# Banded attention and MoE on one core: half of the first k by another queue, v of batch 0 in four loads, and a new order of the first batch's attention

## The chip, the core and the metric

The kernel runs on one core of a Trainium2 chip. The metric is the device time of one execution in microseconds. The kernel before takes 321.01 us (median of three runs, 320.98 to 322.28). Profiles are of one further execution; the one of the kernel before took 319.8 us, of which 318.1 lie between its first and last instruction, with a mean granted TensorE clock of 0.994.

## What is computed

Two layers, one after the other. The first is attention over a local sequence of 512 tokens and 32 global tokens, for 8 batches and 8 heads of dimension 64: global queries see every key, local queries see the global keys and a band of 32 keys to each side. The second is a feed-forward layer of width 2048 with the gate x * sigmoid(1.702 x).

```python
k_all = concat([k_g, k_l]);  v_all = concat([v_g, v_l])
out_g = softmax(scale * q_g @ k_all.T) @ v_all
s_ll  = where(|i - j| <= 32, scale * q_l @ k_l.T, -1e9)
out_l = softmax(concat([scale * q_l @ k_g.T, s_ll])) @ v_all
x     = heads side by side of concat([out_g, out_l])      # 4352 x 512
h     = x @ w_in                                          # 512 x 2048
out   = (h * sigmoid(1.702 * h)) @ w_out                  # 2048 x 512
```

Inputs and output are f32 in DRAM. The kernel computes in bf16 with f32 sums.

## The kernel before

Four heads of one batch make a "quad", so each batch has two: quads 0 and 1 are batch 0. A quad is worked off in steps: `Tk`, `Tq` transpose k and q on VectorE in blocks of 32; `S(rnd)` are the score matmuls of one half of the keys, `X` their exp on ScalarE, `M` the band mask on VectorE; `K` and `XK` are scores and exp for the global keys; `U(0)` sums the rows, `U(1)` and `U(2)` multiply by v; `R` makes the reciprocal of the row sums; `XL` writes the normalised result, which is the operand of the MoE matmuls; `Gm` and `G` do the same for the global queries. The MoE matmuls of w_in are `h_mm` and those of w_out `o_mm`.

Most loads are issued by GpSimd, whose DMAs cast f32 to bf16 on the way. SyncE and ScalarE issue plain copies only. The loads at the start:

```python
def load_k(b, u, j):                      # one of 4 heads of quad u: 32 partitions, 64 KB in bf16
    nc.gpsimd.dma_start(out=loaded[b][0][32 * j : 32 * j + 32, u], in_=kf[b, j][:, u])

def load_v(b, us=(0, 1)):                 # 4 loads each: 64 KB for one quad, 128 KB for both
    s = slice(us[0], us[-1] + 1)
    hs = slice(4 * us[0], 4 * us[-1] + 4)
    for t in (0, 2, 1, 3):
        p = slice(32 * t, 32 * t + 32)
        nc.gpsimd.dma_start(out=vtiles[b % 2][p, s, :, :, :D], in_=vf[b, t][:, hs])

load_g32(0, "qk")                         # q_g, k_g as f32, by SyncE
q32 = ld.tile([128, 16 * D], F32, name="q32", bufs=1)
nc.scalar.dma_start(out=q32, in_=qf[0][:, 0])     # q of quad 0 as f32, by ScalarE
load_g32(0, "v", eng=nc.scalar)
load(0, kq=False)
for j in range(4):
    load_k(0, 0, j)                       # k of quad 0
# ... two affine_selects on GpSimd for the band mask ...
load(0, (1,))                             # k and q of quad 1
# ...
keep(17, psP.tile([128, 512], F32, name="w", tag="p"))    # matmuls on zeros at the start

def load_rest():
    load_v(0, (0,))
    load_v(0, (1,))
    for part in range(2):
        cs = slice(part * (d_ff // 2), (part + 1) * (d_ff // 2))
        for u in range(2):
            nc.gpsimd.dma_start(out=w_in_sb[:, part, 2 * u : 2 * u + 2, :], in_=w_in_r[u][:, :, cs])
    # ... w_out, and k, q and v of batches 1 and 2
```

The loaded half of w_in that belongs to quad 0's result (`kc` 0 and 1) is the first of these four, that of quad 1 (`kc` 2 and 3) the second; the last two are the columns of `fc` 8 to 15. PSUM has eight banks: four in one tile for scores (`psS`, one buffer), four single ones (`psP`), which are used in turn for `kb`, the three `ov`, `og` and later for `hp`.

The order of the first batch:

```python
a, c = Quad(0), Quad(1)
make_mb()
for hf in range(2):
    nc.scalar.activation(rq[:, 0, ...], q32[:, ...], AF.Copy)     # cast q, halves of 512
make_mask()
cast_g32(0, "qk"); transpose_g(0, 2); a.ext()
a.Tq(0, 8); a.Tq(8, 16); a.Tk((0, 1)); a.Tk((2, 3))
load_rest()
a.S(0); a.X(0); expand_g(0, 0)
a.S(1, split=True, warm=4); a.X(1)        # 4 further matmuls on zeros ahead
c.ext(); cast_g32(0, "v"); c.Tk(); expand_g(0, 1)
a.K(); a.XK(); a.M(0); c.Tq()
c.S(0); c.X(0); a.M(1)
load_g32(1, "qkv", hold=True)
a.U(0); a.U(1)
c.S(1); c.X(1)
a.U(2); c.K(); c.XK()
a.Gm(); a.R(); c.M(0); a.XL(0); a.XL(1); c.M(1); a.G()
pt = pts[0] = psS.tile([128, 4, 512], F32, name="s4")
for fc in (0, 1):
    h_mm(0, fc, pt[:, fc, :], (0, 1))     # the first MoE matmuls
for unit in range(3):
    c.U(unit)
for fc in (2, 3):
    h_mm(0, fc, pt[:, fc, :], (0, 1))
c.R(); c.XL(0); c.XL(1); c.Gm()
for kc in (2, 3):
    for fc in range(4):
        h_mm(0, fc, pt[:, fc, :], (kc,))
# ... tanh, c.G(), gate, then fc 4 to 15, then the further batches
```

Of the kernel before, what the change touches and what calls it, by code (L numbers as in the profile page):

```python
# [12 lines left out]
F32 = mybir.dt.float32  # L13
BF16 = mybir.dt.bfloat16
FP8 = mybir.dt.float8e4
AF = mybir.ActivationFunctionType
# [4 lines left out]
def kernel(  # L21
# [12 lines left out]
    nc = tc.nc  # L34

    B, H, Sl, D = q_l.shape
# [20 lines left out]
    ld = ctx.enter_context(tc.tile_pool(name="ld", bufs=3))  # L57
# [7 lines left out]
    kf = k_l.rearrange("b (u j) (c r t) d -> b j r u c (t d)", j=4, c=4, t=4)  # L65
# [7 lines left out]
    def load(b, us=(0, 1), kq=True):  # L73
        if b not in loaded:
            loaded[b] = (ld.tile([128, 2, 4, 4 * D], BF16, name="rk"),
                         ld.tile([128, 2, 16 * D], BF16, name="rq"))
        if kq:
            for j in (0, 2, 1, 3):
                for u in us:
                    load_k(b, u, j)  # L80
            load_q(b, us)

    def load_k(b, u, j):
        nc.gpsimd.dma_start(out=loaded[b][0][32 * j : 32 * j + 32, u], in_=kf[b, j][:, u])  # L84

    def load_q(b, us):
        s = slice(us[0], us[-1] + 1)
        nc.gpsimd.dma_start(out=loaded[b][1][:, s], in_=qf[b][:, s])
# [3 lines left out]
    def load_v(b, us=(0, 1)):  # L92
# [5 lines that stand above are left out]
# [12 lines left out]
    def load_g32(b, names, hold=False, eng=None):  # L110
        for name, s in (("q", qgf), ("k", kgf), ("v", vgf)):
            if name in names:
                t = g32[b, name] = consts.tile([128, 2, D], F32, name="g32%s%d" % (name, b))
                if hold:
                    nc.vector.memset(t[:, :, 0:1], 0.0)
                (eng or nc.sync).dma_start(out=t, in_=s[:, 2 * b : 2 * b + 2, :])

    def cast_g32(b, names):
        for name, t in (("q", rqg), ("k", rkg), ("v", rvg)):
            if name in names:  # L120
                if b:
                    nc.scalar.activation(t[:, 2 * b : 2 * b + 2, :], g32[b, name], AF.Copy)
                else:
                    nc.vector.tensor_copy(t[:, 2 * b : 2 * b + 2, :], g32[b, name])

    load_g32(0, "qk")

    q32 = ld.tile([128, 16 * D], F32, name="q32", bufs=1)
    nc.scalar.dma_start(out=q32, in_=qf[0][:, 0])
    load_g32(0, "v", eng=nc.scalar)  # L130
    load(0, kq=False)
    for j in range(4):
        load_k(0, 0, j)


    mk = consts.tile([32, 208], BF16)
# [1 line left out]
    for sg, base in ((1, 2 * W + 3), (-1, -3)):  # L138
        nc.gpsimd.affine_select(
            out=mk, in_=mk, pattern=[[-sg, 208]], compare_op=ALU.is_ge,  # L140
            fill=0.0, base=base, channel_multiplier=4 * sg,
        )
    load(0, (1,))

    w_in_sb = wts.tile([128, 2, NKC, d_ff // 2], BF16)
    w_out_sb = wts.tile([128, FC, d_model], BF16)
# [24 lines left out]
    def make_mb():  # L171
        for k in range(4):
            nc.vector.tensor_copy(mb[32 * k : 32 * k + 32],
                                  mk[:, 3 - k : 195 - k].rearrange("p (r t) -> p t r", t=16))

    def make_mask():
        at = 0
        for c, (r0, nr) in enumerate(WIN):
            lo = r0 - 8 * c + 2
            nc.scalar.activation(  # L180
                mask[:, c // 2, at : at + 16 * nr].rearrange("p (t r) -> p t r", t=16),
                mb[:, :, lo : lo + nr], AF.Copy)
            at = (at + 16 * nr) % LW
# [7 lines left out]
    for i in range(2):  # L191
        v = consts.tile([128, 2, 4, 4, D + 2], BF16, name="v%d" % i)
# [14 lines left out]
    def transpose_g(lo, hi):  # L207
        for dst, s in ((kgT, rkg), (qgT, rqg)):
            nc.vector.transpose(dst[:, lo:hi, :32], s[:, lo:hi].bitcast(F32))

    def expand_g(b, which):
        qs = slice(2 * b, 2 * b + 2)
        kgBD, vgBD = GB[b % 3]
        out_, in_ = (kgBD, kgT[:, qs].bitcast(BF16)) if which == 0 else (vgBD[:, :, :, :D], rvg[:, qs])
        nc.vector.tensor_mul(
            out_,
            in_.rearrange("p n (o w) -> p n o w", o=1).to_broadcast([128, 2, 4, D]),
            bdm.rearrange("p (o j) w -> p o j w", o=1).to_broadcast([128, 2, 4, D]),
        )

    def load_rest():
        load_v(0, (0,))
        load_v(0, (1,))
        for part in range(2):
            cs = slice(part * (d_ff // 2), (part + 1) * (d_ff // 2))
            for u in range(2):
                nc.gpsimd.dma_start(out=w_in_sb[:, part, 2 * u : 2 * u + 2, :], in_=w_in_r[u][:, :, cs])
        for g4 in range(4):
            nc.gpsimd.dma_start(
                out=w_out_sb[:, 4 * g4 : 4 * g4 + 4, :].rearrange("p (g e) m -> p g (e m)", e=2),  # L230
                in_=w_out_r[:, 2 * g4 : 2 * g4 + 2, :])
            if g4 == 1:
                load(1, (0,))
        load(1, (1,))
        load_v(1, (0,))
        load_v(1, (1,))
        load(2)
# [173 lines left out]
    def width(i):  # L411
        return TB if i < B else B * Sg
# [3 lines left out]
    def h_mm(i, fc, hp, kcs):  # L416
        for kc in kcs:
            nc.tensor.matmul(hp[:, : width(i)], lhsT=w_in_c[:, fc // 8, kc, fc % 8 // 2, :, fc % 2],  # L418
                             rhs=(xL[i] if i < B else xG)[:, kc, :],
                             start=(kc == 0), stop=(kc == NKC - 1))  # L420
# [45 lines left out]

    a, c = Quad(0), Quad(1)
    rk, rq = loaded[0]
    make_mb()
    for hf in range(2):  # L470
        nc.scalar.activation(rq[:, 0, 512 * hf : 512 * hf + 512], q32[:, 512 * hf : 512 * hf + 512], AF.Copy)
    make_mask()
    cast_g32(0, "qk")
    transpose_g(0, 2)
    a.ext()
    a.Tq(0, 8)
    a.Tq(8, 16)
    a.Tk((0, 1))
    a.Tk((2, 3))
    load_rest()  # L480
    a.S(0)
    a.X(0)
# [1 line left out]
    a.S(1, split=True, warm=4)  # L484
    a.X(1)
    c.ext()
    cast_g32(0, "v")
    c.Tk()
    expand_g(0, 1)
    a.K()  # L490
    a.XK()
    a.M(0)
    c.Tq()
    c.S(0)
    c.X(0)
    a.M(1)
    load_g32(1, "qkv", hold=True)
    a.U(0)
    a.U(1)
    c.S(1)  # L500
    c.X(1)
    a.U(2)
    c.K()
    c.XK()
    a.Gm()
    a.R()
    c.M(0)
    a.XL(0)
    a.XL(1)
    c.M(1)  # L510
    a.G()
    gTs[0] = moe.tile([128, FC, TB], BF16, name="gT")
    pt = pts[0] = psS.tile([128, 4, 512], F32, name="s4")
    for fc in (0, 1):
        h_mm(0, fc, pt[:, fc, :], (0, 1))
    for unit in range(3):
        c.U(unit)
    for fc in (2, 3):
        h_mm(0, fc, pt[:, fc, :], (0, 1))
    c.R()  # L520
    c.XL(0)
    c.XL(1)
    c.Gm()
    for kc in (2, 3):
        for fc in range(4):
            h_mm(0, fc, pt[:, fc, :], (kc,))
    th4 = th4s[0] = ld.tile([128, 4, TB], F32, name="th4", bufs=1)

    def tanh2(hf):
# [24 lines left out]
    a, c = nq[1]  # L554
# [37 lines left out]
    a, c = nq[2]  # L592
# [116 lines left out]
```

The softmax here doesn't subtract the row's maximum and nothing guards it: scores larger than these inputs give would overflow.

## Time and profile before

| | |
|---|---|
| time, median of three | 321.01 us |
| span of the profiled execution | 318.1 us |
| TensorE (PE) busy | 305.9 us, 96% |
| VectorE (DVE) busy | 214.9 us, 68% |
| ScalarE (ACT) busy | 165.9 us, 52% |
| GpSimd (POOL) busy | 81.0 us, 25% |
| first score matmul | 8.34 us |
| first v load issued by GpSimd | 7.34 us |
| first w_in load issued by GpSimd | 12.58 us |
| first MoE matmul | 20.52 us |

The profile counts time from the first instruction. Issuing a DMA takes time on the engine that issues it; the data land later. A row of the timeline merges equal instructions that follow each other, and gives in brackets how long the engine was idle ahead of it and what ended that. Matmuls with output `s` are scores on line 297, and on line 418 the first four column blocks of the MoE, since both use the same PSUM tile. Idle time of TensorE counts here: its busy share is 96%, and it is at nine tenths or more in every slice from the fifth to the last but one.

### The profile page before, as it was taken

The numbers are of one execution on the slowest core, as the hardware profiler recorded it, in microseconds if no ns is written. First come the engines' busy times: TensorE is split into PE (matmuls) and PEld (weight loads), VectorE is DVE, ScalarE is ACT, GpSimd is POOL, SyncE is SP. The second block draws the span as 40 slices with busy tenths as digits, with TensorE's granted clock in tenths as the row PEclk, the third lists the DMA queues.
The fourth block names the chain that finished last, engine by engine and source line by source line (L and its number), as shares of the span: only waits on it lengthen the run. The fifth ranks groups of instructions, "written<-read, shape, count | busy, mean of one in ns | idle before, by whom it ended". The sixth has DMA issues, their size and how long they took to land.

```text
span 318.1 us, 7343 instructions
## 1 busy us (share of the span) xinstructions
PE 305.9 (96%) x2997; PEld 148.3 (47%) x2997; DVE 214.9 (68%) x467; ACT 165.9 (52%) x252; POOL 81.0 (25%) x133
## 2 busy tenths in 40 slices
PE   8759999999999999999999999999999999999994
PEld 2424444544554455444454455445454454445651
DVE  8847876978865876677866876687758855573320
ACT  4723765276446744565536735564546642563421
POOL 8932579585136000910045001200000000000000
PEclk9989999999999999999999999999999999999999
DMA  8999999999959211970269111900110011101122
GB/s 155 125 169 209 207 155 174 176 150 126 154 79 172 40 34 44 142 116 1 68 69 179 22 35 51 116 2 20 48 44 26 2 35 51 50 0 34 35 66 66
DMA packets 59904, 27.40 MB, mean 86 GB/s; under 512 B 43232, under 2 KB 51424, under 8 KB 59872
## 3 DMA queue, kind: packets, MB, share of 16 engines
q0 software_dynamic: 51568, 17.11, 50.4%
q1 hardware_dynamic: 7888, 9.25, 10.7%
q10 hardware_dynamic: 416, 0.59, 0.6%
q8 instruction: 23, 0.38, 0.5%
q14 instruction: 9, 0.07, 0.1%
HBM read 35.13 MB, written 8.91 MB: 138 GB/s over the span
## 4 chain that ended last, share of the span: by engine, by line
PE 89%; POOL 3%; DMA 2%; DVE 2%; ACT 1%; issue 1%; POOLq 0%; DVEq 0%; ACTq 0%
PE op L443 36%; PE hp L418 35%; PE s L297 5%; PE ov L353 4%; PE ov L345 4%; DMA w_in_sb<-in_moe_w_in_dram 2%; PE kb L330 2%; POOL v L97 2%; POOL rk L84 1%; PE s L418 1%; PE og L371 1%; PE s L306 1%; DVE sT L377 0%; DVE gT L462 0%; ACT th L425 0%
## 5 line engine op out<-in xcount | busy, mean ns | idle before, releaser
L443 PE MATMUL op<-w_out_sb,gT 128*128 128x512 bf16 x544 | 125.2, 379 | 0.4 <-DVE xL L386 0.4
L426 DVE SCALAR_TENSOR_TENSOR gT<-th,hp 128x512 bf16<-128x512 f32 (+1 forms) x140 | 91.1, 656 | 47.4 <-ACT th L425 46.8
L418 PE MATMUL hp<-xL,w_in_sb 128*128 128x512 bf16 x496 | 108.5, 379 | 0.0
L425 ACT ACTIVATE th<-hp 128x512 f32<-128x512 f32 (+1 forms) x140 | 79.8, 573 | 42.5 <-PE hp L418 39.4
L418 PEld LDWEIGHTS <-w_in_sb 128*128 128x128 bf16 x576 | 56.1, 98 | 67.6 <-DMA w_in_sb<-in_moe_w_in_dram 3.6
L443 PEld LDWEIGHTS <-gT 128*128 128x128 bf16 x544 | 51.9, 98 | 61.0 <-issue 3.6
L318 ACT ACTIVATE e<-s 128x1712 bf16<-128x1712 f32 x31 | 49.5, 1597 | 29.3 <-PE s L297 25.4
L97 POOL DMA_DIRECT2D v<-in_v_l_dram x40 | 28.9, 730 | 95.9 <-PE og L371 91.0
L450 ACT ACTIVATE ob<-op 128x512 f32<-128x512 f32 x34 | 20.3, 597 | 62.8 <-PE op L443 62.8
L84 POOL DMA_DIRECT2D rk<-in_k_l_dram x64 | 34.9, 553 | 17.3 <-DMA w_in_sb<-in_moe_w_in_dram 6.3
L325 DVE TENSOR_TENSOR e<-e,mask 128x1408 bf16<-128x1408 bf16 x32 | 28.0, 874 | 11.1 <-ACT e L318 11.0
L377 DVE STREAM_TRANSPOSE sT<-ov 128x512 f32<-128x512 f32 x16 | 11.4, 714 | 25.3 <-PE ov L353 25.3
L297 PE MATMUL s<-q,kT 32*128 32x200 bf16 (+1 forms) x512 | 21.2, 283 | 1.5 <-DVE q L270 0.7
L386 DVE TENSOR_TENSOR xL<-ov,rs 128x512 bf16<-128x512 f32 x32 | 20.6, 685 | 1.5
L297 PEld LDWEIGHTS <-kT 32*128 32x128 bf16 x512 | 10.8, 95 | 11.7 <-issue 7.5
L353 PE MATMUL ov<-e,v 128*32 128x192 bf16 (+1 forms) x512 | 15.6, 243 | 0.0
L353 PEld LDWEIGHTS <-v 128*32 128x32 bf16 x512 | 12.1, 99 | 3.7 <-issue 0.5
L345 PE MATMUL ov<-ek,vgBD 128*32 128x512 bf16 x128 | 12.9, 393 | 0.3 <-DVE sT L377 0.3
L381 DVE STREAM_TRANSPOSE rs<-rT 128x512 f32<-128x512 f32 x16 | 11.4, 712 | 0.5
L267 DVE STREAM_TRANSPOSE kT<-rk 128x512 f32<-128x512 f32 (+1 forms) x17 | 11.3, 668 | 0.0
L270 DVE STREAM_TRANSPOSE q<-rq 128x512 f32<-128x512 f32 (+1 forms) x17 | 10.8, 643 | 0.1
L330 PE MATMUL kb<-q,kgBD 128*128 128x512 bf16 x32 | 9.8, 388 | 0.5 <-ACT e L316 0.5
(64 smaller groups left out, 149.5 us busy)
## 6 DMA issues: line engine op xcount, KB each, us to landing
out_dram<-ob SPq DMA_DIRECT2D x136, 64.0 KB, 1.9
rk<-in_k_l_dram POOLq DMA_DIRECT2D x64, 64.0 KB, 4.0
rq<-in_q_l_dram POOLq DMA_DIRECT2D x6, 512.0 KB, 6.8
v<-in_v_l_dram POOLq DMA_DIRECT2D x24, 128.0 KB, 4.4
w_in_sb<-in_moe_w_in_dram POOLq DMA_DIRECT2D x4, 512.0 KB, 12.3
w_out_sb<-in_moe_w_out_dram POOLq DMA_DIRECT2D x4, 512.0 KB, 13.4
v<-in_v_l_dram POOLq DMA_DIRECT2D x16, 64.0 KB, 3.7
rq<-in_q_l_dram POOLq DMA_DIRECT2D x3, 256.0 KB, 7.9
```

The costliest lines, as they stand in the source:

```text
L84: nc.gpsimd.dma_start(out=loaded[b][0][32 * j : 32 * j + 32, u], in_=kf[b, j][:, u])
L97: nc.gpsimd.dma_start(out=vtiles[b % 2][p, s, :, :, :D], in_=vf[b, t][:, hs])
L297: nc.tensor.matmul(ps[j][:, off : off + n * nr], lhsT=self.k[p, 128 * c : 128 * c + 128, e], rhs=self.q[p, t0 : t0 + n, r0 : r0 + nr, e], ...
L318: nc.scalar.activation(e[:, :, :RW], self.ps[:, :, :RW], AF.Exp, scale=scale)
L325: nc.vector.tensor_mul(e, e, mask[:, rnd : rnd + 1, :].to_broadcast([128, 4, LW]))
L345: nc.tensor.matmul(ov[32 * j : 32 * j + 32, :], lhsT=lv, rhs=self.ek, start=True, stop=False, skip_group_check=True)
L353: nc.tensor.matmul(ov[32 * j : 32 * j + 32, :].rearrange("p (t r) -> p t r", t=16)[:, :, r0 : r0 + nr], lhsT=lv, rhs=self.E[c // 2][:, j, ...
L386: nc.vector.tensor_mul(self.x[:, 2 * self.u + h, :], self.st[1 + h], self.st["rs"])
L418: nc.tensor.matmul(hp[:, : width(i)], lhsT=w_in_c[:, fc // 8, kc, fc % 8 // 2, :, fc % 2], rhs=(xL[i] if i < B else xG)[:, kc, :], start=( ...
L425: nc.scalar.activation(th[:, :n], hp[:, :n], AF.Tanh, scale=0.851)
L426: nc.vector.scalar_tensor_tensor(gTs[i][:, fc, :n], in0=th[:, :n], scalar=1.0, in1=hp[:, :n], op0=ALU.add, op1=ALU.mult)
L443: nc.tensor.matmul(op, lhsT=gTs[i][:, fc, tci * 128 : tci * 128 + 128], rhs=w_out_sb[:, fc, :], start=(first and fc == 4 * f4), stop=(fc = ...
```

## The change

K of quad 0 no longer comes through GpSimd with a cast, but as f32 through SyncE's queue, in four loads; ScalarE casts one half of its columns and VectorE the other. The small global q and k move from SyncE's queue to ScalarE's, behind q. The eight v loads of batch 0 become four of twice the size. GpSimd thereby has fewer loads to issue before those of w_in. The order of the first batch is changed as well: both score rounds of quad 1 come ahead of the products of quad 0 with v, all of quad 1's U ahead of the first MoE matmuls, and the global results (`G`, `Gm` of quad 1) behind them.

```diff
-    load_g32(0, "qk")
-
+    load(0, kq=False)
     q32 = ld.tile([128, 16 * D], F32, name="q32", bufs=1)
+    k32 = ld.tile([128, 4, 4 * D], F32, name="k32", bufs=1)
     nc.scalar.dma_start(out=q32, in_=qf[0][:, 0])
-    load_g32(0, "v", eng=nc.scalar)
-    load(0, kq=False)
     for j in range(4):
-        load_k(0, 0, j)
+        nc.sync.dma_start(out=k32[32 * j : 32 * j + 32], in_=kf[0, j][:, 0])
+    load_g32(0, "qk", eng=nc.scalar)
+    load_g32(0, "v")
+    for j in range(4):
+        load_k(0, 1, j)
 # ... affine_selects
-    load(0, (1,))
+    load_q(0, (1,))
 # ... in load_rest()
-        load_v(0, (0,))
-        load_v(0, (1,))
+        load_v(0)
 # ... the order of batch 0; cast_q(hf) is the former loop's body
     make_mb()
-    for hf in range(2):
-        nc.scalar.activation(rq[:, 0, ...], q32[:, ...], AF.Copy)
+    cast_q(0)
+    cast_q(1)
+    nc.scalar.activation(rk[:, 0, 2:4], k32[:, 2:4], AF.Copy)
     make_mask()
     cast_g32(0, "qk")
     transpose_g(0, 2)
     a.ext()
+    nc.vector.tensor_copy(rk[:, 0, 0:2], k32[:, 0:2])
     a.Tq(0, 8)
+    a.Tk((0, 1))
     a.Tq(8, 16)
-    a.Tk((0, 1))
     a.Tk((2, 3))
 # ... load_rest, a.S(0), a.X(0), expand_g, a.S(1), a.X(1)
     c.ext()
-    cast_g32(0, "v")
-    c.Tk()
-    expand_g(0, 1)
+    c.T()
     a.K()
     a.XK()
     a.M(0)
-    c.Tq()
     c.S(0)
     c.X(0)
+    cast_g32(0, "v")
+    expand_g(0, 1)
     a.M(1)
     load_g32(1, "qkv", hold=True)
     a.U(0)
-    a.U(1)
+    c.K()
+    c.XK()
+    a.R()
     c.S(1)
     c.X(1)
+    a.U(1)
     a.U(2)
-    c.K()
-    c.XK()
     a.Gm()
-    a.R()
     c.M(0)
+    c.M(1)
     a.XL(0)
     a.XL(1)
-    c.M(1)
-    a.G()
 # ... gTs[0], pt
-    for fc in (0, 1):
-        h_mm(0, fc, pt[:, fc, :], (0, 1))
     for unit in range(3):
         c.U(unit)
-    for fc in (2, 3):
+    c.R()
+    for fc in range(4):
         h_mm(0, fc, pt[:, fc, :], (0, 1))
-    c.R()
     c.XL(0)
     c.XL(1)
-    c.Gm()
     for kc in (2, 3):
         for fc in range(4):
             h_mm(0, fc, pt[:, fc, :], (kc,))
+    a.G()
+    c.Gm()
```

## The prediction

> **What bounds the kernel now.** I read the slices first (TensorE at nine tenths or more from the fifth slice on), then the list of TensorE's waits, the timeline of the first 28 us, and the same stretch in windows. One TensorE wait is far longer than the rest:
>
> ```profile
> PE s L418 <- DMA w_in_sb<-in_moe_w_in_dram: 3.4, 1, 3.4
> PE w L155 <- DVE warm L151: 1.5, 1, 1.5
> PE s L297 <- DVE q L270: 0.7, 1, 0.7
> ...
> PE ov L345 <- DVE sT L377: 0.3, 1, 0.3
> ```
>
> TensorE is busy 305.9 of 318.1 us, and only 0.7 us of named waits lie after 27 us (0.3 on sT, 0.4 on xL). Whatever is won must therefore be won before the first MoE matmuls. In the timeline (start, length, engine, line, what, in brackets the idle time ahead and its releaser):
>
> ```profile
> 1.35 2.29 POOL L84 DMA_DIRECT2D rk<-in_k_l_dram  x4 [0.84 <-POOLq L693]
> ...
> 4.52 2.27 POOL L84 DMA_DIRECT2D rk<-in_k_l_dram  x4
> ...
> 7.34 5.25 POOL L97 DMA_DIRECT2D v<-in_v_l_dram  x8
> ...
> 8.34 0.66 PE L297 MATMUL s<-q,kT 32*128 32x200 bf16 x16 [0.17 <-DVE kT L267]
> ...
> 12.58 2.80 POOL L227 DMA_DIRECT2D w_in_sb<-in_moe_w_in_dram  x4
> ...
> 20.52 1.50 PE L418 MATMUL s<-xL,w_in_sb 128*128 128x512 bf16 x4 [3.43 <-DMA w_in_sb<-in_moe_w_in_dram]
> ```
>
> GpSimd issues without a pause from 1.35 us, and reaches w_in only at 12.58. The weights land 7.9 us later, and TensorE has run out of attention work by then. It stands still until 20.52, and pays twice: the windows show what the clock did (length, then busy time per engine, PEclk, DMA share, GB/s):
>
> ```profile
> 18.00:20.00 2.00, 0.00 (x0) 0.00 (x0) 0.93 (x4) 0.00 (x0) 0.00 (x0) 1.00 1.01 159
> 20.00:22.00 2.00, 1.48 (x8) 0.41 (x12) 0.00 (x0) 0.00 (x0) 0.55 (x1) 0.74 1.14 209
> 22.00:24.00 2.00, 2.00 (x45) 1.46 (x48) 0.76 (x2) 0.00 (x0) 0.00 (x0) 0.50 1.13 205
> 24.00:26.00 2.00, 2.00 (x52) 0.91 (x40) 1.86 (x4) 0.00 (x0) 0.54 (x1) 0.91 1.13 206
> ```
>
> Lost clock: 2 x (0.26 + 0.50 + 0.09) = 1.7 us. So at most 3.4 + 1.7 = 5.1 us hang on this one transfer. The last of the 16 first MoE matmuls (two halves of w_in over four column blocks) ends at 27.9 us; from there on TensorE is full. I predict how far that moment moves.
>
> **What the Trainium skill says.** "TensorE: Matmul & The Clock Gate", Part 1, says that an idle window of about 3.4 us puts the array on half its clock, until a busy window of that length has passed. The trace agrees: 3.43 us of idleness, then clock 0.50. "DMA: Bandwidth & Descriptors", Issuing engines are not separate DMA queues: a load from another queue uses the same 16 DMA engines and saves only issue time. The trace shows those engines loaded from 4 us on (DMA share 1.0 to 2.1 per window), so I don't count the earlier issue in full. "VectorE: DVE Perf Modes", What auto-detection actually checks: a one-source operation between SBUF tensors can run two elements per cycle; by that the new 128x512 cast might take half of what one element per cycle would. The trace has only 128x128 casts, at 0.22 to 0.35 us, which don't decide it.
>
> **The change, part by part.**
>
> 1. *GpSimd's issue time.* Four k loads leave its queue (2.27 us). Eight v loads of 64 KB become four of 128 KB. The eight took 5.25 us; the later 128 KB v loads take 0.78 us each, so four take 3.1: 2.1 us less. w_in is issued at about 12.6 - 2.3 - 2.1 = 8.2 us.
>
> 2. *The DMA engines.* What lies ahead of w_in stays almost the same in bytes read: k's first half merely comes as f32, 512 KB written instead of 256. v's rows arrive as 128-byte packets, 0.52 MB, and the windows from 10 to 14 us move 117 to 143 GB/s while it is at work, so v needs about 4 us however it is issued, beginning when q of quad 1 is in. I put that at 7.5 to 8 us instead of about 10, and v's end at about 12 instead of 14.7. So w_in's data move 2.5 us earlier (1.6 to 3.4), not 4.4. In the timeline GpSimd[...] is let go by w_in at 20.76, 24.79, 27.65 and 30.16; these stand for the four landings. After: about 18.2, 22.3, 25.2, 27.7.
>
> 3. *The front.* q32 (512 KB on ScalarE's queue) now shares the engines with k32, and q_g and k_g are second and third on ScalarE's queue instead of first and second on SyncE's. Before, ScalarE began its cast of q at 4.72, and VectorE its cast of q_g at 5.96 without a wait. I estimate both small tensors and k32 at 6.3 to 7 us: up to 0.3 us of wait. VectorE gets one more cast (128x512, f32 to bf16) ahead of the transposes: 0.35 to 0.6 us, I take 0.5. The three transposes ahead of the first scores stay three. The first scores start at 8.34 + 0.3 + 0.5 = **9.15 us**. ScalarE's added cast (0.61 us, as its q casts) lies in its idle time before the first exp.
>
> 4. *The middle, TensorE's new order.* Times from the rows of before. exp of quad 0, first half: 9.85 to 11.45 (1.60). c.T is moved up on VectorE and its data are on the chip sooner, so its two 0.71 us transposes end at 11.75; then the mask (0.9) to 12.65. exp, second half: 11.45 to 13.2 (1.81, overlapped a little); mask to 14.15; exp of the kg scores to 13.75. Scores of quad 1 start at 12.5 on TensorE, the row sums of quad 0 (U 0) at 13.9, ended by the mask at 14.6. exp of quad 1: 13.75 to 15.3; kg exp to 15.9; second scores of quad 1 at 15.35 to 16.25; exp to 18.1. TensorE fills this time with U 1, U 2 and Gm of quad 0 (0.8 + 0.8 + 0.5), to 18.4. VectorE: mask of quad 1 at 17.95 to 18.85, then the two xL products (1.3) to 20.15. Quad 1's U 0 ends at 19.3; U 1 and U 2 need the PSUM banks that the xL products free (19.5, 20.15) and end at 21.2. ScalarE and VectorE thus set the pace here; TensorE loses about 1 us in small gaps, none near 3.4 us.
>
> 5. *The first MoE matmuls.* Eight on quad 0's xL: 21.2 to 22.95 (0.216 each). They want the first w_in at 21.2, and it is there at 18.2. VectorE meanwhile: R of quad 1 (1.7) to 21.85, xL to 22.5 and 23.15. The last eight run 22.95 to 24.7 and want the second w_in, there at 22.3. G of both quads now comes after them, and Gm of quad 1 is put behind (0.5). Equal work is done at **25.2 us instead of 27.9: 2.7 us less**. The next two w_in pieces are wanted at about 25.2 + 4 x 0.87 = 28.7, and the last is there at 27.7.
>
> Afterwards nothing changes in kind: the later streams move by 2.5 us, TensorE's demand by 2.7. 321.0 - 2.7 = **318.3 us**, 0.8% less.
>
> **Rivals.** (a) *The wait only moves*: w_in comes no earlier, as the DMA engines are the limit. For it: DMA shares of 1 and over from 4 us on. Against: in 6 to 10 us they move only 127 to 134 GB/s while GpSimd is at full issue, so issue limits there. Even then the first w_in (20.5) is in time for the new order, while the second (24.8) and the last (30.2) are 1.8 us late: about 320 us. (b) *The front gets dearer than counted*: k32 or k_g land at 8 us; the scores start at 10, and the chain through exp shifts by as much: 319 to 319.5. (c) *ScalarE and VectorE are not as tight as I laid them*, or later starts overlap better: up to 4.5 us gained, 316.5. (d) *The DMA queue falls behind later*, at q and v of batch 1 (v lands late, U at 51 us wants it): some tenths of a us back.
>
> **Range and chances.** The middle is 318.3. (a), (b) and (d) pull up by 1 to 1.7, (c) down by 1.5; eight in ten lie in 316.9 to 319.9. Over 2% faster would be under 314.6, more than the 5.1 us at stake plus the small gaps: 0.02. Over 2% slower would take a new wait of 6 us that nothing points to: 0.01. Within 2%: 0.97.
>
> **What the profile after would show.** Right: no TensorE wait for w_in over 0.5 us, and no clock of 0.50 after the start; the v issues in one row of four, about 3.1 us; w_in issued near 8.2; first scores near 9.15; a cast of k on VectorE of about 0.5 us; the last matmul on L418 with output s at about 24.7 and more exp-bound gaps ahead of it. Wrong: a wait for w_in in front of the second eight matmuls or at the eighth column block (rival a); VectorE idle before 7.5 us on k32 or k_g (rival b); waits for v or rq between 38 and 60 us (rival d).

## The result and the profile after

The changed kernel takes **319.5 us** (median of four runs, 319.07 to 319.67) against 321.01. The ratio is 0.9941, with a 95% interval of 0.9915 to 0.9968; it is estimated from the runs of both kernels and is not the quotient of these two medians (0.9953). The predicted 318.3 lay below the result, the range of 316.9 to 319.9 holds it. The gain was 1.5 us by the medians, 1.9 by the ratio (1.0 to 2.7 over its interval), instead of 2.7. TensorE no longer waits for w_in, as predicted, but the front of the kernel became longer than predicted.

TensorE's waits of the changed kernel, longest first (the columns are total us, times, longest):

```profile
PE s L298 <- DVE q L271: 2.8, 1, 2.8
PE w L157 <- DVE warm L153: 1.5, 1, 1.5
PE ov L354 <- DVE e L326: 0.9, 1, 0.9
PE ov L346 <- ACT ek L337: 0.6, 1, 0.6
```

The wait for w_in is gone. In its place stands one of 2.8 us ahead of the first scores. The timeline of the changed kernel shows both ends of the trade:

```profile
5.08 3.22 POOL L97 DMA_DIRECT2D v<-in_v_l_dram  x4
...
7.86 0.49 DVE L124 CAST rkg<-g32k 128x128 bf16<-128x128 f32 x1 [1.04 <-DMA g32k<-in_k_g_dram]
...
8.47 2.81 POOL L228 DMA_DIRECT2D w_in_sb<-in_moe_w_in_dram  x4 [0.17 <-issue]
...
8.61 0.63 ACT L477 ACTIVATE rk<-k 128x512 bf16<-128x512 f32 x1 [2.10 <-DMA k<-in_k_l_dram]
...
9.18 0.42 DVE L482 CAST rk<-k 128x512 bf16<-128x512 f32 x1
...
10.65 0.90 PE L298 MATMUL s<-q,kT 32*128 32x200 bf16 x16 [2.76 <-DVE q L271]
...
11.49 1.89 PE L157 MATMUL s<-warm 128*128 128x512 bf16 x4
...
23.49 3.63 PE L419 MATMUL s<-xL,w_in_sb 128*128 128x512 bf16 x16
```

GpSimd reaches w_in at 8.47 instead of 12.58 us. But k_g has landed only at 7.86 and k, as f32, at 8.61; VectorE's casts and transposes follow, and the first scores start at 10.65 instead of 8.34. TensorE, whose zero matmuls end at 7.9, is idle for 2.76 us, and the windows (length, busy time per engine, PEclk, DMA share, GB/s) show the clock that follows:

```profile
8.00:10.00 2.00, 0.00 (x0) 0.00 (x0) 1.93 (x10) 1.39 (x5) 1.83 (x4) 1.00 1.51 187
10.00:12.00 2.00, 1.34 (x18) 0.81 (x19) 2.00 (x9) 0.59 (x2) 1.48 (x3) 0.54 2.42 154
12.00:14.00 2.00, 2.00 (x21) 0.61 (x20) 1.59 (x3) 1.20 (x1) 1.76 (x3) 0.61 1.67 195
14.00:16.00 2.00, 1.39 (x24) 0.63 (x21) 0.79 (x4) 1.94 (x5) 0.56 (x2) 1.00 1.13 212
```

The half clock, which before lay in the windows from 20 to 26 us, now lies in those from 10 to 14: the first scores take 0.90 us instead of 0.66, the four zero matmuls 1.89 instead of 1.04. So the column blocks from fc 4 on, which started at 27.77 us before, start at 27.33 in this profile. This pair of profiles shows a smaller gain than the medians do: 0.2 us (319.8 to 319.61). The profiled execution of the kernel before is 1.2 us faster than its median. Its mean clock was 0.994; in 39 further runs of that kernel the clock lay between 0.982 and 0.995, with a median of 0.989, so most of them lose more to the clock than the profile shows.

### The profile page after: what moved, and what is told of

It reads as the page before. It is cut to its first block, busy times and chain, and to the rows that moved or that the text cites. A ratio compares the mean times of both kernels' runs of the same rounds, so it can differ in the third digit from the quotient of the medians.

```text
span 317.9 us, 7344 instructions
## 1 busy us (share of the span) xinstructions
PE 305.5 (96%) x2997; PEld 148.0 (47%) x2997; DVE 216.0 (68%) x468; ACT 166.5 (52%) x253; POOL 77.1 (24%) x125
## 4 chain that ended last, share of the span: by engine, by line
PE 84%; DMA 10%; POOL 2%; DVE 1%; issue 1%; ACT 0%; POOLq 0%; DVEq 0%
PE op L444 36%; PE hp L419 33%; DMA w_out_sb<-in_moe_w_out_dram 6%; PE s L298 5%; PE ov L354 4%; PE ov L346 3%; PE kb L331 2%; DMA v<-in_v_l_dram 2%; DMA rq<-in_q_l_dram 2%; POOL rk L84 1%; PE og L372 1%; PE s L307 1%; DVE sT L378 0%; POOL mk L141 0%; DVE rs L382 0%
## 5 line engine op out<-in xcount | busy, mean ns | idle before, releaser
L319 ACT ACTIVATE e<-s 128x1712 bf16<-128x1712 f32 x31 | 49.6, 1599 | 27.9 <-PE s L298 24.5
L97 POOL DMA_DIRECT2D v<-in_v_l_dram x36 | 27.1, 765 | 97.7 <-PE og L372 93.7
L84 POOL DMA_DIRECT2D rk<-in_k_l_dram x60 | 32.7, 556 | 15.9 <-DVE rT L380 3.2
```

Source lines behind the costliest of these rows:

```text
L319: nc.scalar.activation(e[:, :, :RW], self.ps[:, :, :RW], AF.Exp, scale=scale)
```

## The experiments

Ratios are to the kernel before, run beside them on the same chip, with 95% intervals. "hp" is the start of the column blocks from fc 4 on, the moment that the prediction was about; the kernel before has it at 27.77 us, the changed one at 27.33. First scores and hp are read from one profile each; the time of that execution stands beside them, and need not be near the median.

| kernel | first scores, us | hp, us | profiled run, us | median, us | ratio (95%) |
|---|---|---|---|---|---|
| changed kernel | 10.65 | 27.33 | 319.61 | 319.5 | 0.9941 (0.9915 to 0.9968) |
| keep29 | 10.10 | 25.37 | 322.16 | 319.73 | 0.9955 (0.9933 to 0.9977) |
| warm_late | 10.65 | 25.92 | 318.38 | 318.34 | 0.9905 (0.9883 to 0.9926) |
| g_first | 10.60 | 27.02 | 319.67 | 319.47 | 0.9943 (0.9918 to 0.9968) |
| order_before | 9.89 | 24.91 | 317.26 | 319.24 | 0.9926 (0.9893 to 0.9959) |
| order_before_keep | 10.29 | 25.32 | 318.89 | 319.38 | 0.9937 (0.9914 to 0.9959) |
| order_only | 8.34 | 26.35 | 321.61 | 321.07 | 0.9974 (0.9944 to 1.0004) |
| k_gpsimd | 8.32 | 26.12 | 318.18 | 318.2 | 0.9898 (0.9858 to 0.9939) |
| k_gpsimd_warm | 8.32 | 24.92 | 316.96 | 317.88 | 0.9880 (0.9846 to 0.9913) |
| before_keep | 8.34 | 26.76 | 318.81 | 319.08 | 0.9916 (0.9887 to 0.9946) |
| v4_only | 8.33 | 26.26 | 318.28 | 317.73 | 0.9875 (0.9845 to 0.9905) |
| v4_warm | 8.32 | 25.10 | 317.69 | 317.57 | 0.9867 (0.9836 to 0.9897) |

Two things help to read the table. Five of its kernels start with the same loads and casts (the changed kernel, keep29, warm_late, order_before, order_before_keep), and their first scores lie between 9.89 and 10.65 us: the front varies by 0.76 us from profile to profile. And in nine of the twelve profiles, and in that of the kernel before, the span from the first to the last instruction is hp plus 290.3 to 291.0 us. Behind hp something else was lost in keep29 (295.1), order_before_keep (291.8) and order_only (293.5).

**Is the half clock what cost the rest?** Theory 1 says that the front gave back what w_in won. The first test covers the gap ahead of the first scores with more matmuls on zeros:

```diff
-    keep(17, psP.tile([128, 512], F32, name="w", tag="p"))
+    keep(29, psP.tile([128, 512], F32, name="w", tag="p"))
```

> The changed kernel with 29 instead of 17 matmuls on zeros at the start, which reach to about 10.6 us instead of 7.9. Theory 1 (the front lost what w_in won: k as f32 and k_g land near 8 us, TensorE stands idle for 2.8 us, and a window at half clock follows): the first scores stay at 10.65, but no clock of 0.5 after them; the four zero matmuls take 1.0 instead of 1.9 us, the first scores 0.66 instead of 0.90; about 1.1 us less, 318.4. Theory 2 (the front has slack, and the chain through exp and masks or the new order itself sets the end): within 0.3 us of 319.5.

The start did what theory 1 says, from first scores that came 0.55 us earlier than expected: no half clock before 27 us, zero matmuls ahead of the second scores at 1.04 us, hp at 25.37. The median stayed at 319.73, although four of the 22 runs took 318.30 to 318.33, near the expected 318.4. In the profiled execution, with 322.16 us one of the three slowest, something later gave the time back. TensorE's waits name a new one, and its timeline shows where:

```profile
PE og L372 <- issue: 2.4, 1, 2.4
```

```profile
54.41 0.30 PE L372 MATMUL og<-v,e 128*32 128x66 bf16 x15
57.15 0.20 PE L372 MATMUL og<-v,e 128*32 128x66 bf16 x1 [2.44 <-issue]
```

TensorE stops between the 15th and the 16th of equal matmuls, with nothing that it waits for in the record, and the mean clock from 58 to 68 us is 0.87. Whether such stops are also what holds the median up is not shown. keep29 has 24 instructions more on TensorE than the changed kernel, so it was repeated with the same number, by starting the 17 zero matmuls later:

```diff
-    nc.vector.memset(warm, 0.0)
-    keep(17, psP.tile([128, 512], F32, name="w", tag="p"))
 # ... behind VectorE's other memsets and the copies into vgBD
+    nc.vector.memset(warm, 0.0)
+    keep(17, psP.tile([128, 512], F32, name="w", tag="p"))
```

> The changed kernel with the same 17 matmuls on zeros, started later: the memset of their operand stands behind VectorE's other memsets, so they run from about 4.4 to about 10 us instead of 1.5 to 7.9. TensorE has exactly the instructions of the changed kernel, unlike keep29, which has 24 more. Theory 1 (the shortfall of the changed kernel is the late front with its half clock): the idle gap ahead of the first scores falls below 1 us, no half clock from 10.4 to 13.9, the column blocks from fc 4 on start at 25.4 to 26 instead of 27.3, 318 us. If TensorE again loses 1 to 3 us between 50 and 58 us with nothing named that it waits for, as in keep29 and order_before_keep: 319.5, and the stall does not depend on the number of instructions.

This separates the late front from the clock. The first scores start at 10.65 us, just as late as in the changed kernel, but after an idle time of 0.99 us and at full clock:

```profile
4.21 5.46 PE L156 MATMUL w<-warm 128*128 128x512 bf16 x17 [4.21 <-DVE warm L206]
...
10.65 0.66 PE L298 MATMUL s<-q,kT 32*128 32x200 bf16 x16 [0.99 <-DVE q L271]
11.24 1.04 PE L156 MATMUL s<-warm 128*128 128x512 bf16 x4
```

hp falls to 25.92 and the time to 318.34 us, ratio 0.9905: with nothing changed but when the zero matmuls run. That this is nearly the predicted 318.3 is chance, as hp is 0.7 us later than the predicted 25.2. The stop near 55 us is absent in the profile. The half clock alone is thus 1.4 us of hp (27.33 - 25.92); in the medians it is 1.2 us. The run times of the two kernels don't overlap (from 319.07 and up to 318.93), the intervals of their ratios still do (0.9915 and 0.9926).

**Why do k and k_g land so late?** Two kernels separate the possible reasons. The first puts the small loads ahead of k on SyncE's queue:

```diff
+    load_g32(0, "qk")
     for j in range(4):
         nc.sync.dma_start(out=k32[32 * j : 32 * j + 32], in_=kf[0, j][:, 0])
-    load_g32(0, "qk", eng=nc.scalar)
```

> The changed kernel with q_g and k_g first on SyncE's queue, ahead of k as f32. Theory 1a (at the front k_g, which lands at 7.9 us, is what VectorE waits for): k_g is there at about 6, and the first scores start near 9.2 if k then comes in time. Theory 1b (the f32 copy of k, there at 7.8 to 8.6 us, is the wait that ends last): VectorE waits for k instead, and the first scores stay at 9.9 to 10.4. In time: 1a 318 to 318.5, 1b within 0.5 us of the changed kernel.

Theory 1b holds. VectorE casts q_g and k_g at 6.07 and 6.22, and then waits for k, which is now the last to come:

```profile
6.22 0.22 DVE L124 CAST rkg<-g32k 128x128 bf16<-128x128 f32 x1
...
9.12 0.43 DVE L482 CAST rk<-k 128x512 bf16<-128x512 f32 x1 [1.50 <-DMA k<-in_k_l_dram]
...
10.60 0.66 PE L298 MATMUL s<-q,kT 32*128 32x200 bf16 x16 [3.45 <-DVE q L271]
```

The first scores stay at 10.60, the ratio at 0.9943. Either order leaves one of them late. TensorE is now idle for 3.45 us, and the half clock lasts twice as long, from 12.1 to 18.9 us. It does not cost twice as much: from the first scores to hp this profile takes 16.42 us, the changed kernel 16.68 with a half clock of 3.4 us, and warm_late 15.27 without one. So the cost of a half clock is not fixed by its length. The second kernel keeps GpSimd's own loads back until k is there:

```diff
+    nc.gpsimd.affine_select(
+        out=k32[:, 0, 0:16], in_=k32[:, 0, 0:16], pattern=[[1, 16]], compare_op=ALU.is_ge,
+        fill=0.0, base=1, channel_multiplier=0,
+    )
     for j in range(4):
         load_k(0, 1, j)
```

> The changed kernel, in which GpSimd touches k32 (an affine_select that keeps every value) ahead of its first load, so that its loads start only when k as f32 has landed. The question is why k as f32 lands at 7.8 to 8.6 us. Theory A (its packets share the DMA engines with those of GpSimd's k loads of quad 1 and with q32): with GpSimd's loads away k lands at 6 to 6.5, and k_g with it. Theory B (the copies from SyncE's queue are slow by themselves, 512 packets of 1 KB behind q32): k lands at 7.8 to 8.6 as before. The whole is later either way, as every GpSimd load waits; the time is not the point.

```profile
7.53 0.20 POOL L134 TENSOR_SCALAR_AFFINE_SELECT k<-k 128x16 f32<-128x16 f32 x1 [7.02 <-DMA k<-in_k_l_dram]
```

k lands at 7.5 us, as GpSimd's select is released by it, and k_g at 7.3 (issued at 1.73, 5.6 us to landing). In the five profiles with GpSimd's loads ScalarE's cast of k, which waits for it, starts at 7.98 to 8.61 us, and VectorE's cast of k_g, which waits too, at 7.02 to 8.12. So sharing with GpSimd's loads explains 0.5 to 1.1 us of k, and nothing that can be seen of k_g. Neither theory got its number: even without those loads k is 1 us later than theory A said. What delays it then is not shown; the 512 KB of q on ScalarE's queue, under way at the same time, are a candidate. (One run, 324.46 us, as everything on GpSimd waits; its time says nothing more.)

**What is each part worth?** k by GpSimd as before, with the rest of the change kept:

```diff
-        nc.sync.dma_start(out=k32[32 * j : 32 * j + 32], in_=kf[0, j][:, 0])
+        load_k(0, 0, j)
 # ... q_g, k_g on SyncE, v_g on ScalarE as before; load(0, (1,)) for quad 1; both casts of k removed
```

> The changed kernel with k of quad 0, q_g, k_g and v_g loaded as in the kernel before (GpSimd with cast; small ones first on SyncE), but v in four loads and the new order. Theory 1: first scores back at 8.3 to 8.6 us without an idle gap, w_in issued at about 10.4 and there at about 18, which the new order wants only at about 20.4; the 16 first MoE matmuls end at about 24.4; 316.6 us, so k by SyncE costs about 3 us. Theory 2 (front has slack): 319 to 319.5. Theory 3 (w_in has to be issued as early as in the changed kernel): a wait for w_in and about 319.

The first scores are back at 8.32, and w_in, issued at 10.44, is no wait. The time, 318.2 us, is 1.3 us better than the changed kernel's, less than the 3 us expected, and the intervals overlap (0.9939 and 0.9915). hp at 26.12 says why: there are new gaps.

```profile
12.14 0.71 DVE L269 STREAM_TRANSPOSE q<-rq 128x512 f32<-128x512 f32 x1 [2.12 <-DMA rq<-in_q_l_dram]
...
12.90 0.70 PE L296 MATMUL s<-q,kT 32*128 32x200 bf16 x16 [1.35 <-DVE q L269]
```

VectorE waits 2.1 us for q of quad 1, TensorE 1.4 us for VectorE and later 0.9 us, and its clock is halved from 13.4 to 20.2 us (the expectation below has 13.7 to 20.5). The same with zero matmuls in TensorE's two gaps:

```diff
-    c.S(0)
+    c.S(0, warm=6)
-    a.U(0)
+    a.U(0, warm=4)
```

> k_gpsimd (k by GpSimd, v in four loads, new order) with 6 matmuls on zeros ahead of the first scores of quad 1 and 4 ahead of U 0 of quad 0, in the gaps of 1.35 and 0.87 us that TensorE has there; k_gpsimd showed half clock from 13.7 to 20.5 us. Theory: no half clock, U 1 and U 2 of quad 0 take 0.8 us each instead of 1.4, the MoE matmuls end about 1.5 us earlier, 316.5 to 317. Rival (exp and masks set the pace there, the clock is hidden): within 0.5 us of k_gpsimd's 318.2.

hp falls to 24.92, the profile's clock stays at 1.0, and U 1 and U 2 take the short times. The median moves by 0.3 us only; the theory expected 1.2 to 1.7. In the pair of profiles hp is better by 1.2 us and the span by 1.3 (316.5 to 315.2). But only two of the six runs, the profiled one among them, took about 316.96 us; the other four took 317.66 to 318.21. What they lose, and where, is not known.

k_gpsimd with v in eight loads again has only the order left of the change:

```diff
-        load_v(0)
+        load_v(0, (0,))
+        load_v(0, (1,))
```

> As k_gpsimd, but v of batch 0 in eight loads again: of the change only the new order is left. Theory 1: w_in issued at about 12.6, there at 20.5 when it is wanted at 20.4, the second piece at 24.8 when it is wanted at 22.2; a wait of 2 to 2.6 us for it, in all 318.5 to 319.5, 2 to 2.5 us behind k_gpsimd. Rival (the order alone is the gain, the v loads do nothing): equal to k_gpsimd within 0.4 us.

321.07 us, ratio 0.9974: the order alone gains nothing that can be told from zero, about 2.9 us behind k_gpsimd. The expected form of the wait was wrong: w_in came in pieces that the new order mostly met, at 21.6 and 24.5 us, and only 0.2 us of a named wait for it is left. Of the 3.4 us between the two profiled spans (319.9 and 316.5) only 0.2 are there at hp (26.35 and 26.12), although TensorE stops ahead of it for 1.1 us with nothing named:

```profile
22.16 0.42 PE L353 MATMUL ov<-e,v 128*32 128x192 bf16 x12 [1.10 <-issue]
```

The other 3.1 us are lost behind hp. There TensorE waits 0.9 us for the gate, 0.8 for w_out, 0.3 for q and 0.2 for w_in, of which k_gpsimd has none; this accounts for about 2.3 us. Why w_out is late stays open. The reverse, the changed kernel's loads with the former order:

```diff
-    c.T()
+    cast_g32(0, "v"); c.Tk(); expand_g(0, 1)
 # ... and all further steps of batch 0 as in the kernel before
```

> The changed kernel's loads and casts with the order of steps of the kernel before. Theory 1 (with w_in early and the front late, the order matters little): no wait for w_in, 318.8 to 320. Rival (the new order is what turns the early w_in into time): 320.5 to 321.5, as TensorE then waits for exp and masks instead of w_in.

319.24 us, 0.9926 (0.9893 to 0.9959): theory 1. Against the changed kernel's 0.9941 the new order shows no gain. The profiled execution is the fastest of the ten (317.26 us), with hp at 24.91. It has nearly the gap of the changed kernel, and yet its mean clock was 1.0; in the other runs it lies between 0.98 and 1.0.

```profile
9.89 0.66 PE L298 MATMUL s<-q,kT 32*128 32x200 bf16 x16 [2.65 <-DVE q L271]
```

With 29 zero matmuls:

> order_before (the changed kernel's loads, the former order) with 29 matmuls on zeros at the start, as in keep29. If the order is worth nothing with w_in early, the span is that of order_before's undisturbed profile, 315.6, in most runs: 317.2 to 317.7. If the former order needs the half clock's absence as little as keep29 did, and something after 27 us gives it back: 319 to 319.7.

The second expectation came true: 319.38 us with hp at 25.32, and again TensorE stops at the same line near 55 us, with nothing named:

```profile
55.49 0.21 PE L372 MATMUL og<-v,e 128*32 128x66 bf16 x2 [1.07 <-issue]
```

Finally two single lines on the kernel before. The four v loads alone:

```diff
-        load_v(0, (0,))
-        load_v(0, (1,))
+        load_v(0)
```

> The kernel before with v of batch 0 in four loads and nothing else. First scores at 8.3. w_in issued at about 10.4 and there at about 19.4, as in k_gpsimd, while TensorE is ready for it at 17.0: a wait of about 2.4 instead of 3.4 us. Theory 1 (the early w_in is worth its shift, 1.1 us, and the half clock stays or goes by chance): 318.5 to 320. Rival (the new order is needed to turn it into time): 320.5 to 321.5.

317.73 us, **0.9875** (0.9845 to 0.9905): this one line beats the whole change (the two intervals don't overlap), and is better than I expected. Its timeline shows the gain and a cost that I had not seen:

```profile
10.44 2.86 POOL L226 DMA_DIRECT2D w_in_sb<-in_moe_w_in_dram  x4
...
16.36 0.78 PE L352 MATMUL ov<-e,v 128*32 128x160 bf16 x16 [1.75 <-DMA v<-in_v_l_dram]
...
19.00 0.54 POOL L84 DMA_DIRECT2D rk<-in_k_l_dram  x1 [1.90 <-DMA w_in_sb<-in_moe_w_in_dram]
```

w_in lands at 19.0 instead of about 20.8, and TensorE never waits for it. In its stead it waits 1.75 us for v, since a load now carries both quads and quad 0's U 1 needs the whole; the clock is halved from 16.0 to 19.4 us (16.3 to 19.7 in the last expectation below). And the kernel before with its wait filled:

```diff
     keep(17, ...)
 # ... on the kernel before, 15 zero matmuls in the wait for w_in
+    keep(15, pt[:, 0, :])
     for fc in (0, 1):
         h_mm(0, fc, pt[:, fc, :], (0, 1))
```

> The kernel before with 15 matmuls on zeros in the wait for w_in (17.2 to 20.5 us); no load and no step is moved. The first MoE matmul stays at 20.5. If the half clock after the wait costs what its windows show (1.7 us), the clock stays at 1.0 there and the time falls by 1.5 to 2 us, to about 319.4. Rival (the lost clock is hidden behind VectorE's chain or the later w_in loads): within 0.5 us of before.

319.08 us, 0.9916 (0.9887 to 0.9946). No transfer is earlier, the first MoE matmul starts at 20.71, and still 2 us are won by the medians: the clock is what the wait had cost beyond itself. The mean clock of its six runs is 0.997 to 0.999, that of the 16 runs of the kernel before beside it 0.987 to 0.994. Against the one profile of the kernel before, itself a fast execution, hp and span move by 1.0 us only (27.77 to 26.76, 318.1 to 317.1).

v4_only with zero matmuls in its own two gaps:

```diff
-    c.S(0)
+    c.S(0, warm=6)
-    a.U(1)
+    a.U(1, warm=7)
```

> v4_only with matmuls on zeros in its two waits: 6 ahead of the first scores of quad 1 (1.3 us for q of quad 1), 7 ahead of U 1 of quad 0 (1.8 us for v). Theory: the half clock seen from 16.3 to 19.7 us in v4_only goes, the 16 first MoE matmuls end about 0.8 us earlier, 317.0. Rival (the wait for w_in takes what the clock gives): 317.5 to 318, as v4_only.

317.57 us, 0.9867 (0.9836 to 0.9897). The half clock is gone and hp is at 25.10, but the step from v4_only is within the noise, as the rival said. It is the fastest median of all, together with v4_only and k_gpsimd_warm, which can't be told from it.

## Why the prediction was right or wrong

1. *GpSimd's issue time*: right. v in 3.22 us (3.1 predicted), w_in at 8.47 (8.2).

2. *The DMA engines*: wrong, but on the safe side. I gave w_in 2.5 us of the 4.4 by which I expected its issue to move, as I took the engines for the limit. GpSimd is let go by w_in at these times:

```profile
16.25 0.55 POOL L84 DMA_DIRECT2D rk<-in_k_l_dram  x1 [1.19 <-DMA w_in_sb<-in_moe_w_in_dram]
18.74 0.55 POOL L84 DMA_DIRECT2D rk<-in_k_l_dram  x1 [1.94 <-DMA w_in_sb<-in_moe_w_in_dram]
23.19 0.55 POOL L88 DMA_DIRECT2D rq<-in_q_l_dram  x1 [3.91 <-DMA w_in_sb<-in_moe_w_in_dram]
25.83 0.71 POOL L230 DMA_DIRECT2D w_out_sb<-in_moe_w_out_dram  x1 [2.09 <-DMA w_in_sb<-in_moe_w_in_dram]
```

That is 4.3 to 6.1 us earlier than before (20.76, 24.79, 27.65, 30.16): more than the issue moved (4.1). From 14 to 16 us the engines now move 212 GB/s, where they moved 103 before. This is more than was needed: the first piece is there 7 us before TensorE asks for it, and in v4_only, where it comes at 19.0, TensorE doesn't wait for it either. Rival (a) is refuted.

3. *The front*: **the step that failed.** Predicted: small tensors and k at 6.3 to 7 us, a wait of up to 0.3, first scores at 9.15 (the sum as written is 9.14). Measured: k_g at 7.86, k at 8.61, waits of 0.39 and 1.04 us on VectorE, first scores at 10.65, 1.5 us later than predicted; in the other profiles with these loads they are 0.7 to 1.5 us later. VectorE's waits, 1.43 us instead of 0.3, make up 1.1 of the 1.5. The cast itself was sized right (0.42 us, 0.5 taken). The prediction did say that the queues share the DMA engines, but took too little for it. g_first shows that k_g is late through its place behind q on ScalarE's queue: ahead of k on SyncE's queue it no longer keeps VectorE waiting. For k, k_alone shows 0.5 to 1.1 us that come from GpSimd's loads; the rest stays open. This is rival (b), for which the text said 319 to 319.5.

4. *The clock at the front*: the prediction expected no clock of 0.50 after the start, and looked for gaps near 3.4 us only in the middle. The late front made one of 2.76, and in this execution it was enough. warm_late takes away this alone, and gets 318.34.

5. *The middle*: right in length. From the first scores to the first MoE matmul I laid out 12.05 us; the changed kernel takes 12.84 with its half clock, warm_late 11.36 without. But the new order is not what paid. With w_in early and at full clock the way from the first scores to hp takes 15.27 us in the new order (keep29, warm_late) and 15.02 and 15.03 us in the former one (order_before, order_before_keep).

6. *After the start*: nothing is given back in the changed kernel (290.6 us from hp to the end, 290.3 before), rival (d) did not come. Why TensorE stops in keep29 and order_before_keep at 55 us stays open. The stop lies within a row of equal matmuls. Both have 24 instructions more than the kernel with the same order of steps. But before_keep has 30 more than its own and v4_warm 26, and neither stops in its profile, while order_only has no added matmul and stops at 22 us for 1.10 us. So the number of instructions does not explain it.

So the gain hoped for from w_in was real. The change paid for it at the front with 2.3 us of start, and with a half clock of 3.4 us that the prediction had counted as won. That the time still lies in the range is partly luck: in the pair of profiles hp moved by 0.4 us where 2.7 were predicted, and the profiled executions are 0.2 us apart. The other 1.3 of the 1.5 us in the medians lie in runs of the kernel before of which there is no profile.

## What to carry to other kernels

Before moving a load to another queue to relieve the first, ask what the load itself is the head of: k opened the whole chain, w_in had a slack of some us, and merging eight small v loads into four won the slack without touching k. Count an idle gap of TensorE with the half clock that may follow it: zero matmuls in a wait that could not be shortened won 2 us (before_keep), and starting them later won about 1.2 (warm_late). It is not a sure gain: in keep29, order_before_keep, k_gpsimd_warm and v4_warm zero matmuls filled gaps as well, and the medians moved by 0.3 us at most. When two parts of a change pull at the same wait, run each alone; here one line was worth more than the whole.

## What the runs showed that I had not expected

The length of a gap does not decide alone whether the clock halves. The changed kernel was idle for 2.76 us, and its clock was halved from 10.14 us on; order_before was idle for 2.65 us, and its clock stayed. k_gpsimd had no TensorE wait over 1.4 us, and its clock was still halved, from 13.4 us on. Apart from those that begin in the last microseconds, the half clocks of all profiles last 3.41 us or a multiple of it, so I cut each trace into stretches of that length, from its first record of the clock on. These are stretches of the changed kernel, k_gpsimd and v4_only, then two of order_before (TensorE alone; length, busy, PEclk, DMA share, GB/s):

```profile
6.73:10.14 3.41, 1.16 (x6) 1.00 1.49 194
9.95:13.36 3.41, 1.59 (x36) 1.00 2.72 148
12.59:16.00 3.41, 1.51 (x40) 1.00 1.65 164
5.42:8.83 3.41, 1.82 (x9) 1.00 1.26 217
8.83:12.24 3.41, 2.35 (x38) 1.00 2.39 158
```

After the first three, with TensorE busy for 34, 47 and 44% of the stretch, the clock was halved; after the two of order_before, 53 and 69%, it was not. Up to 300 us this holds in all 14 profiles: a stretch at full clock with at most 47% was followed by a half clock, one with 53% or more was not. Near the end of three traces a stretch of 43 to 48% was not followed by one, so it is an observation and no rule. It says that the same gap may or may not cost clock, depending on how it falls into the stretches.

The Trainium skill ("TensorE: Matmul & The Clock Gate", Part 1) speaks of an idle window of about 3.4 us. The length fits, but here TensorE did not have to be idle for all of it, and the measurement decides. I had relied on that figure in the fourth part of the prediction.

And the price of issuing grows slowly with the size of a load: a v load of 64 KB holds GpSimd for 0.64 us, one of 128 KB for 0.78.
